# Transposes by the DMA crossbar in place of TensorE: a linear-attention and gated-FFN kernel on one core

## The chip, the core and the metric

The kernel runs on one core of a Trainium2 chip. The core has a matrix engine (TensorE, PE in the profile), a vector engine (VectorE, DVE), an activation engine (ScalarE, ACT), a general engine (GpSimd, POOL) and a queue engine (SyncE, SP) that issues most transfers; sixteen DMA engines carry them. TensorE writes to the accumulation memory PSUM, from which VectorE or ScalarE must copy; everything else lives in the on-chip memory SBUF. The metric is the device time of one execution in microseconds.

## The reference

Eight heads of a recurrent attention with a decay per head, over four sequences of 768 tokens, then an RMS norm and a gated feed-forward layer (3072 tokens, 512 wide, 1536 inside):

```python
gamma = 1.0 - 2.0 ** (-5.0 - np.arange(H))          # H = 8, D = 64, S = 768, B = 4
for t in range(S):
    state = gamma * state + einsum('bhd,bhe->bhde', k[:, :, t], v[:, :, t])
    y[:, :, t] = (1 / sqrt(D)) * einsum('bhd,bhde->bhe', q[:, :, t], state)
x = y.transpose(0, 2, 1, 3).reshape(B * S, H * D)
xn = x / sqrt(mean(x * x) + 1e-6) * rms_g
g = xn @ w_gate
out = (g / (1 + exp(-g)) * (xn @ w_val)) @ w_out
```

## The kernel before

The sequence is cut into six chunks of 128 tokens. A chunk has four batch rows (b), each a tile of 128 tokens by 512 (eight heads of 64). For one chunk and row the attention is a series of pieces:

- `cast` (L136): q and k from float32 to bfloat16, and v times a decay per token, on GpSimd (q of chunk 0 on VectorE). After it, from chunk 1 on, SP issues the loads of the next chunk's same row (L149).
- `piece_t` (L152): q and k must have the head dimension on the partitions for the scores. Eight TensorE transposes of 128x128 write them to PSUM, and one ScalarE copy brings them back (L159).
- `piece_a` (L163): scores of all heads on TensorE; VectorE masks them on the way out (L173).
- `piece_y` (L178): masked scores times v, plus q times the running state; the update of the state; the output's decay on VectorE (L200), its squares on ScalarE (L204), the inverse norm on GpSimd (`piece_rstd`, L220).
- `piece_n` (L228): the row times its inverse norm, to bfloat16, on VectorE.
- `piece_x` (L234): four TensorE transposes of that row into PSUM; VectorE copies them into the tile `xnT` and multiplies by the gain `rms_g`, which in this layout is one value per partition (L239).

When all four rows of a chunk stand in `xnT`, its FFN (`ffn`, L261) runs in 16 slots: twelve gate/value slots (`gv`: four matmuls each with the two weight matrices, a SiLU on ScalarE, a product on VectorE) and four output slots (`down`: twelve matmuls, a ScalarE copy, a store issued by SP).

The order of the work is written out by hand: every engine runs its instructions in program order. The last loop (L305 to L313) walks through the 16 slots of chunk c's FFN and puts into each slot the attention pieces of chunk c + 1 that a table assigns to it: `PLAN` (L247), or `PLAN1` (L248) for chunk 1. For example `a=(2, 4, 6, 8)` puts the scores of rows 0 to 3 into slots 2, 4, 6 and 8. The prologue (L294 to L304) does the whole attention of chunk 0, with the loads of the weights between. The loads of chunk 1 go out in the first four slots of chunk 0's FFN, each held back until a SiLU of that slot is done.

Buffers: `loads` (L46) has six per tensor, one per chunk and row; `work` (L47) three, unless a tile says otherwise; PSUM is split between attention (`aps`, four) and FFN (`fps`, four). Output copies have three buffers (`ffw`, L48).

Of the kernel before, what the change touches and what calls it, by code (L numbers as in the profile page):

```python
# [9 lines left out]
F32 = mybir.dt.float32  # L10
BF16 = mybir.dt.bfloat16
AX = mybir.AxisListType
AF = mybir.ActivationFunctionType
ALU = mybir.AluOpType
# [3 lines left out]
def kernel(  # L18
# [11 lines left out]
    nc = tc.nc  # L30
    ctx.enter_context(tc.manual_schedule())

    B, H, S, D = q.shape
    C = 128
    NCH = S // C
    NHP = H // 2
    DM = H * D
# [5 lines left out]
    lng = [math.log(1.0 - 2.0 ** (-5.0 - h)) for h in range(H)]  # L43

    const = ctx.enter_context(tc.tile_pool(name="const", bufs=1))
    loads = ctx.enter_context(tc.tile_pool(name="loads", bufs=6))  # L46
    work = ctx.enter_context(tc.tile_pool(name="work", bufs=3))  # L47
    ffw = ctx.enter_context(tc.tile_pool(name="ffw", bufs=3))  # L48
    aps = ctx.enter_context(tc.tile_pool(name="aps", bufs=4, space=bass.MemoryType.PSUM))
# [10 lines left out]
    def load(c, b, after=None):  # L60
        t = []
        for name, src in (("q_f", q), ("k_f", k), ("v_f", v)):
            x = loads.tile([128, H, D], F32, name=name)
            i = nc.sync.dma_start(  # L64
                out=x, in_=src[b].rearrange("h (c p) d -> c p h d", p=C)[c])
            if after is not None:
                tc.add_manual_dep(i.ins, after.ins.name, SYNC_DEP, reason="transfer order")
            t.append(x)
        raw[c, b] = t

    for b in range(B):
# [8 lines left out]
        out=causal, in_=causal, compare_op=ALU.is_ge, fill=0.0, base=0,  # L80
# [19 lines left out]
    nc.scalar.activation(warm, zero, AF.Silu)  # L100
    g_col = const.tile([128, KS], F32, name="g_col")

    def load_g():
        with nc.allow_non_contiguous_dma(reason="one column per 128 entries"):
            nc.gpsimd.dma_start(out=g_col, in_=moe_rms_g.rearrange("(s p) -> p s", p=128))
# [27 lines left out]
    cur = {}  # L133
    mark = {}

    def cast(c, b):  # L136
        q_f, k_f, v_f = raw.pop((c, b))
        qb = work.tile([128, DM], BF16, name="qb")
        kb = work.tile([128, DM], BF16, name="kb")
        vp = work.tile([128, H, D], BF16, name="vp")  # L140
        if c == 0:
            nc.vector.tensor_copy(qb, q_f.rearrange("p h d -> p (h d)"))
        else:
            nc.gpsimd.tensor_copy(qb, q_f.rearrange("p h d -> p (h d)"))  # L144
        nc.gpsimd.tensor_copy(kb, k_f.rearrange("p h d -> p (h d)"))  # L145
        nc.gpsimd.tensor_tensor(  # L146
            out=vp, in0=v_f, in1=vdec[:, c, :, None].to_broadcast([128, H, D]), op=ALU.mult)
        cur[c, b] = dict(qb=qb, kb=kb, vp=vp)
        if 0 < c < NCH - 1:  # L149
            load(c + 1, b)  # L150

    def piece_t(c, b):  # L152
        d = cur[c, b]
        qk_ps = aps.tile([128, 2, NHP, 128], BF16, name="qk_ps", tag="at")
        for i, n in enumerate(("qb", "kb")):
            for hp in range(NHP):
                nc.tensor.transpose(qk_ps[:, i, hp, :], d[n][:, hp * 128:(hp + 1) * 128], ident)  # L157
        qkT = work.tile([128, 2, NHP, 128], BF16, name="qkT")
        nc.scalar.copy(qkT, qk_ps)  # L159
        d["qT"] = qkT[:, 0]  # L160
        d["kT"] = qkT[:, 1]
# [66 lines left out]
    def piece_n(c, b):  # L228
        d = cur[c, b]
        xn = work.tile([128, DM], BF16, name="xn")  # L230
        nc.vector.tensor_scalar_mul(xn, d["x"].rearrange("p h d -> p (h d)"), d["rstd"])  # L231
        d["xn"] = xn

    def piece_x(c, b):  # L234
        xn = cur.pop((c, b))["xn"]
        xt_ps = aps.tile([128, KS, 128], BF16, name="xt_ps", tag="at")
        for s in range(KS):
            nc.tensor.transpose(xt_ps[:, s, :], xn[:, s * 128:(s + 1) * 128], ident)  # L238
        nc.vector.tensor_tensor(  # L239
            out=cur[c, "xnT"][:, :, b * C:(b + 1) * C], in0=xt_ps,  # L240
            in1=g_col[:, :, None].to_broadcast([128, KS, 128]), op=ALU.mult)

    def begin(c):
        cur[c, "xnT"] = work.tile([128, KS, GT], BF16, name="xnT", bufs=2)


    PLAN = dict(cast=(0, 2, 4, 6), t=(1, 3, 5, 7), a=(2, 4, 6, 8), y=(3, 5, 7, 9), n=(6, 8, 10, 13), x=(7, 9, 11, 14))  # L247
    PLAN1 = dict(cast=(5, 7, 9, 11), t=(7, 9, 11, 13), a=(8, 10, 12, 14), y=(9, 11, 13, 15), n=(12, 14, 15, 15), x=(13, 15, 15, 15))  # L248

    def attention(c):  # L250
        s = [[] for _ in range(16)]
        s[0].append(lambda: begin(c))
        plan = PLAN1 if c == 1 else PLAN
        pieces = dict(cast=cast, t=piece_t, a=piece_a, y=piece_y, n=piece_n, x=piece_x)
        for b in range(B):
            for n, f in pieces.items():
                s[plan[n][b]].append(lambda f=f, b=b: f(c, b))
        return s


    def ffn(c):  # L261
        xnT = cur.pop((c, "xnT"))
        hT = ffw.tile([128, NFF, GT], BF16, name="hT", bufs=2)
        slots = []

        def gv(n):
            sl = slice(n * 128, (n + 1) * 128)
            g_ps = fps.tile([128, GT], F32, name="g_ps", tag="ff")
            for s in range(KS):
                nc.tensor.matmul(g_ps, wg_b[:, s, sl], xnT[:, s, :], start=s == 0, stop=s == KS - 1)  # L270
            v_ps = fps.tile([128, GT], F32, name="v_ps", tag="ff")
            for s in range(KS):
                nc.tensor.matmul(v_ps, wv_b[:, s, sl], xnT[:, s, :], start=s == 0, stop=s == KS - 1)  # L273
            sg = ffw.tile([128, GT], BF16, name="sg")
            mark[c, n] = nc.scalar.activation(sg, g_ps, AF.Silu)  # L275
            nc.vector.tensor_tensor(out=hT[:, n, :], in0=sg, in1=v_ps, op=ALU.mult)  # L276

        def down(b):
            o_ps = fps.tile([128, DM], F32, name="o_ps", tag="ff")
            for n in range(NFF):  # L280
                nc.tensor.matmul(o_ps, hT[:, n, b * C:(b + 1) * C], wo_b[:, n, :],  # L281
                                 start=n == 0, stop=n == NFF - 1)
            o_sb = ffw.tile([128, DM], F32, name="o_sb")
            nc.scalar.copy(o_sb, o_ps)  # L284
            nc.sync.dma_start(out=out_v[c, b], in_=o_sb)

        for n in range(NFF):
            slots.append(lambda n=n: gv(n))
        for b in range(B):
            slots.append(lambda b=b: down(b))  # L290
        return slots


    begin(0)  # L294
    P = dict(C=cast, T=piece_t, A=piece_a, Y=piece_y, N=piece_n, X=piece_x, W=lambda c, i: load_w(i), G=lambda c, i: load_g())
    for step in ("C0 T0 C1 G0 A0 T1 Y0 C2 W0 W1 A1 T2 Y1 N0 C3 W2 W3 A2 X0 T3 Y2 N1 A3 X1 Y3 N2 X2").split():
        P[step[0]](0, int(step[1]))
# [3 lines left out]
    for i in range(6):  # L301
        nc.tensor.matmul(hot, ident, st_b[0].rearrange("p a b -> p (a b)"), start=True, stop=True)
    piece_n(0, 3)
    piece_x(0, 3)  # L304
    for c in range(NCH):  # L305
        f_slots = ffn(c)
        a_slots = attention(c + 1) if c + 1 < NCH else [[] for _ in range(16)]
        for i in range(16):
            f_slots[i]()
            if c == 0 and i < B:  # L310
                load(1, i, after=mark[0, i])
            for f in a_slots[i]:
                f()  # L313

# [29 lines left out]
```

## Time and profile before

| | us |
|---|---|
| median of 3 runs | 279.93 (279.19 to 281.76) |
| the profiled execution | 279.49 |
| its span, first to last instruction | 277.8 |
| mean granted TensorE clock | 0.988 |

A profile comes from one execution. Times in its rows are microseconds from the start of the span; `L270` is line 270 of the kernel. A row of a group gives busy time and the mean length of one instruction, then how long the engine had stood idle before and what ended that wait. `PEld` is the loading of weights into TensorE, which overlaps its matmuls. Matmul lengths contain the pipeline's tail, so the distance between starts is what one costs. For SP the length of a DMA instruction is how long it held the queue; the landing is a column of its own. The chain of waits goes back from the last instruction, at each step to what released it.

### The profile page before, as it was taken

How to read it: one execution, taken by the hardware profiler on the slowest of the kernel's cores; microseconds unless marked ns; L12 is line 12 of the kernel's file. 1: busy time of each engine (PE TensorE's matmuls, PEld its weight loads, DVE VectorE, ACT ScalarE, POOL GpSimd, SP SyncE). 2: the span in 40 equal slices, each digit the busy share in tenths (PEclk: the TensorE clock that was granted, in tenths of full speed). 3: DMA queues.
4: the chain of work that ended last, by engine and by line, in shares of the span. 5: the costliest groups of instructions: out<-in, count | busy, mean ns of one | idle time of the engine just before them, and what ended most of it. 6: DMA issues, size and time to landing. Idle time of an engine off the chain costs nothing.

```text
span 277.8 us, 4510 instructions
## 1 busy us (share of the span) xinstructions
PE 246.2 (89%) x1702; PEld 124.4 (45%) x1702; DVE 135.7 (49%) x228; ACT 105.3 (38%) x203; POOL 94.5 (34%) x177
## 2 busy tenths in 40 slices
PE   1567899999299989999989999989999889999994
PEld 0344344455244544445454445544444444444441
DVE  0547134755616778117778027777036664023300
ACT  8546133433124432243432244333144333143311
POOL 6698104662342735303726204627104411000000
PEclk9999999999869999999999999999999999999999
DMA  8999999999898000149900279700200000200012
GB/s 160 218 179 203 204 196 223 212 226 199 246 222 169 0 2 0 76 126 223 182 2 1 108 164 220 119 1 2 113 38 2 0 2 0 113 38 4 0 58 93
DMA packets 84197, 30.17 MB, mean 109 GB/s; under 512 B 75472, under 2 KB 81104, under 8 KB 84176
## 3 DMA queue, kind: packets, MB, share of 16 engines
q1 hardware_dynamic: 78336, 25.17, 42.8%
q0 software_dynamic: 5840, 4.72, 11.0%
q8 instruction: 13, 0.21, 0.4%
q14 instruction: 8, 0.07, 0.1%
HBM read 28.31 MB, written 6.29 MB: 125 GB/s over the span
## 4 chain that ended last, share of the span: by engine, by line
PE 51%; DVE 15%; ACT 9%; DMA 8%; POOL 6%; issue 6%; SPq 3%; ACTq 0%; POOLq 0%; DVEq 0%
PE o_ps L281 21%; PE g_ps L270 13%; PE v_ps L273 12%; DVE am L173 5%; DMA k_f<-in_k_dram 4%; DVE hT L276 3%; SPq L64 3%; ACT xsq L204 3%; DVE x L200 3%; ACT qkT L159 3%; ACT sg L275 3%; DVE xn L231 2%; DMA v_f<-in_v_dram 2%; DVE xnT L239 2%; PE xt_ps L238 2%
## 5 line engine op out<-in xcount | busy, mean ns | idle before, releaser
L276 DVE TENSOR_TENSOR hT<-sg,v_ps 128x512 bf16<-128x512 bf16 x72 | 49.4, 686 | 80.3 <-PE v_ps L273 55.4
L270 PE MATMUL g_ps<-xnT,wg_b 128*128 128x512 bf16 x288 | 76.3, 388 | 1.6 <-DVE xnT L239 1.6
L273 PE MATMUL v_ps<-xnT,wv_b 128*128 128x512 bf16 x288 | 75.7, 386 | 0.0
L275 ACT ACTIVATE sg<-g_ps 128x512 bf16<-128x512 f32 x72 | 43.0, 597 | 59.9 <-PE g_ps L270 59.9
L281 PE MATMUL o_ps<-wo_b,hT 128*128 128x512 bf16 x288 | 64.3, 379 | 0.0
L273 PEld LDWEIGHTS <-wv_b 128*128 128x128 bf16 x288 | 28.6, 99 | 35.3 <-issue 2.2
L222 POOL TENSOR_SCALAR ms<-ssq 128x1 f32<-128x1 f32 x24 | 5.1, 212 | 111.3 <-ACT xsq L204 111.2
L281 PEld LDWEIGHTS <-hT 128*128 128x128 bf16 x288 | 27.6, 98 | 31.4
L270 PEld LDWEIGHTS <-wg_b 128*128 128x128 bf16 x288 | 26.3, 100 | 29.5 <-issue 4.7
L284 ACT COPY o_sb<-o_ps 128x512 f32<-128x512 f32 x24 | 14.1, 586 | 55.6 <-PE o_ps L281 50.5
L173 DVE TENSOR_TENSOR am<-a_ps,causal 128x512 bf16<-128x512 f32 x48 | 30.8, 682 | 3.7 <-PE a_ps L169 3.7
L239 DVE TENSOR_TENSOR xnT<-xt_ps,g_col 128x512 bf16<-128x512 bf16 x24 | 16.5, 686 | 30.9 <-PE xt_ps L238 30.9
L204 ACT ACTIVATE xsq<-x 128x512 f32<-128x512 f32 x24 | 15.1, 630 | 42.7 <-DVE x L200 42.4
L159 ACT COPY qkT<-qk_ps 128x1024 bf16<-128x1024 bf16 x24 | 24.0, 999 | 10.2 <-PE qk_ps L157 10.2
L146 POOL TENSOR_TENSOR vp<-v_f,vdec 128x512 bf16<-128x512 f32 x24 | 24.9, 1039 | 2.3 <-DMA v_f<-in_v_dram 2.3
L200 DVE TENSOR_TENSOR x<-y_ps,ydec 128x512 f32<-128x512 f32 x24 | 16.4, 684 | 5.1 <-PE y_ps L186 5.0
L144 POOL CAST qb<-q_f 128x512 bf16<-128x512 f32 x20 | 12.8, 640 | 15.0 <-DMA q_f<-in_q_dram 14.1
L186 PE MATMUL y_ps<-vp,am 128*128 128x64 bf16 x192 | 13.1, 202 | 4.5 <-DVE am L173 4.5
L145 POOL CAST kb<-k_f 128x512 bf16<-128x512 f32 x24 | 15.2, 635 | 4.5 <-DMA k_f<-in_k_dram 4.5
L169 PE MATMUL a_ps<-qkT 64*128 64x128 bf16 x192 | 10.4, 233 | 6.7 <-ACT qkT L159 6.1
L231 DVE TENSOR_SCALAR xn<-x,rstd 128x512 bf16<-128x512 f32 x24 | 15.6, 649 | 1.1 <-POOL rstd L225 1.1
L238 PE MATMUL xt_ps<-ident,xn 128*128 128x128 bf16 x96 | 10.5, 238 | 5.4 <-DVE xn L231 5.4
(43 smaller groups left out, 159.7 us busy)
## 6 DMA issues: line engine op xcount, KB each, us to landing
q_f<-in_q_dram SPq DMA_DIRECT2D x24, 256.0 KB, 5.1
k_f<-in_k_dram SPq DMA_DIRECT2D x24, 256.0 KB, 5.0
v_f<-in_v_dram SPq DMA_DIRECT2D x24, 256.0 KB, 5.1
out_dram<-o_sb SPq DMA_DIRECT2D x24, 256.0 KB, 2.0
wg_b<-in_moe_w_gate_dram POOLq DMA_DIRECT2D x4, 384.0 KB, 8.3
wv_b<-in_moe_w_val_dram POOLq DMA_DIRECT2D x4, 384.0 KB, 9.1
wo_b<-in_moe_w_out_dram POOLq DMA_DIRECT2D x3, 512.0 KB, 13.2
g_col<-in_moe_rms_g_dram POOLq DMA_DIRECT2D x1, 2.0 KB, 4.2
```

The lines of the kernel that those rows point to most:

```text
L146: nc.gpsimd.tensor_tensor(out=vp, in0=v_f, in1=vdec[:, c, :, None].to_broadcast([128, H, D]), op=ALU.mult)
L159: nc.scalar.copy(qkT, qk_ps)
L173: nc.vector.tensor_tensor(out=am[:, i], in0=a_ps[i], in1=causal[:, None, :].to_broadcast([128, NHP, 128]), op=ALU.mult)
L200: nc.vector.tensor_tensor(out=x, in0=y_ps, in1=ydec[:, c, :, None].to_broadcast([128, H, D]), op=ALU.mult)
L204: nc.scalar.activation(xsq, x.rearrange("p h d -> p (h d)"), AF.Square, accum_out=ssq)
L231: nc.vector.tensor_scalar_mul(xn, d["x"].rearrange("p h d -> p (h d)"), d["rstd"])
L239: nc.vector.tensor_tensor(out=cur[c, "xnT"][:, :, b * C:(b + 1) * C], in0=xt_ps, in1=g_col[:, :, None].to_broadcast([128, KS, 128]), op=AL ...
L270: nc.tensor.matmul(g_ps, wg_b[:, s, sl], xnT[:, s, :], start=s == 0, stop=s == KS - 1)
L273: nc.tensor.matmul(v_ps, wv_b[:, s, sl], xnT[:, s, :], start=s == 0, stop=s == KS - 1)
L275: mark[c, n] = nc.scalar.activation(sg, g_ps, AF.Silu)
L276: nc.vector.tensor_tensor(out=hT[:, n, :], in0=sg, in1=v_ps, op=ALU.mult)
L281: nc.tensor.matmul(o_ps, hT[:, n, b * C:(b + 1) * C], wo_b[:, n, :], start=n == 0, stop=n == NFF - 1)
```

## The change

From chunk 2 on, q and k are not transposed on TensorE: right after the casts, SP issues two DMA transposes through the crossbar, from the cast tile in SBUF to a transposed tile in SBUF. `piece_t` does nothing there, and the PSUM tile and the ScalarE copy fall away. From chunk 1 on, the normalised row goes the same way: `piece_n` multiplies by the inverse norm and by the gain in one VectorE instruction (`scalar_tensor_tensor`), and SP issues a transpose straight into `xnT`; `piece_x` does nothing there. For this the gain is needed along the free dimension on all partitions, so a tile `g_bc` is loaded once by a broadcast, in slot 4 of the first FFN stage. Chunk 0, and q and k of chunk 1, stay as they were.

The tables change: all four casts come in slots 0 to 3 and the scores from slot 4 on. The loads go out two chunks ahead, in slots 5, 7, 9 and 11, no longer from `cast`. Load buffers go from six to eight, those of the cast tiles from three to six.

```diff
-    loads = ctx.enter_context(tc.tile_pool(name="loads", bufs=6))
+    loads = ctx.enter_context(tc.tile_pool(name="loads", bufs=8))
...
+    g_bc = const.tile([128, DM], F32, name="g_bc")
...
-        qb = work.tile([128, DM], BF16, name="qb")
-        kb = work.tile([128, DM], BF16, name="kb")
-        vp = work.tile([128, H, D], BF16, name="vp")
+        qb = work.tile([128, DM], BF16, name="qb", bufs=6)
+        kb = work.tile([128, DM], BF16, name="kb", bufs=6)
+        vp = work.tile([128, H, D], BF16, name="vp", bufs=6)
...
-        if 0 < c < NCH - 1:
-            load(c + 1, b)
+        if c > 1:
+            d = cur[c, b]
+            for n in "qk":
+                t = work.tile([128, NHP, 128], BF16, name=n + "T", bufs=6)
+                nc.sync.dma_start_transpose(out=t, in_=d[n + "b"])
+                d[n + "T"] = t
 
     def piece_t(c, b):
+        if c > 1:
+            return
...
         xn = work.tile([128, DM], BF16, name="xn")
-        nc.vector.tensor_scalar_mul(xn, d["x"].rearrange("p h d -> p (h d)"), d["rstd"])
+        x = d["x"].rearrange("p h d -> p (h d)")
+        if c > 0:
+            nc.vector.scalar_tensor_tensor(out=xn, in0=x, scalar=d["rstd"], in1=g_bc,
+                                           op0=ALU.mult, op1=ALU.mult)
+            nc.sync.dma_start_transpose(out=cur[c, "xnT"][:, :, b * C:(b + 1) * C], in_=xn)
+            return
+        nc.vector.tensor_scalar_mul(xn, x, d["rstd"])
...
     def piece_x(c, b):
-        xn = cur.pop((c, b))["xn"]
+        d = cur.pop((c, b))
+        if c > 0:
+            return
+        xn = d["xn"]
...
-    PLAN = dict(cast=(0, 2, 4, 6), t=(1, 3, 5, 7), a=(2, 4, 6, 8), y=(3, 5, 7, 9), n=(6, 8, 10, 13), x=(7, 9, 11, 14))
-    PLAN1 = dict(cast=(5, 7, 9, 11), t=(7, 9, 11, 13), a=(8, 10, 12, 14), y=(9, 11, 13, 15), n=(12, 14, 15, 15), x=(13, 15, 15, 15))
+    PLAN = dict(cast=(0, 1, 2, 3), t=(1, 3, 5, 7), a=(4, 6, 8, 10), y=(5, 7, 9, 11), n=(7, 9, 11, 13), x=(8, 10, 12, 14))
+    PLAN1 = dict(cast=(5, 7, 9, 11), t=(7, 9, 11, 13), a=(8, 10, 12, 14), y=(9, 11, 13, 15), n=(11, 13, 15, 15), x=(13, 15, 15, 15))
...
             if c == 0 and i < B:
                 load(1, i, after=mark[0, i])
+            if c == 0 and i == 4:
+                nc.sync.dma_start(out=g_bc, in_=moe_rms_g.partition_broadcast(128))
+            if c < NCH - 2 and i in (5, 7, 9, 11):
+                load(c + 2, (i - 5) // 2)
```

## The prediction

> **What bounds the kernel now.** I read the page first, then busy time by stage, then what TensorE waits for in the stages, then the chain of waits around the one stage boundary that looks different. The page:
>
> ```profile
> span 277.8 us, 4510 instructions
> ...
> PE 246.2 (89%) x1702; PEld 124.4 (45%) x1702; DVE 135.7 (49%) x228; ACT 105.3 (38%) x203; POOL 94.5 (34%) x177
> ...
> PE 51%; DVE 15%; ACT 9%; DMA 8%; POOL 6%; issue 6%; SPq 3%; ACTq 0%; POOLq 0%; DVEq 0%
> ```
>
> TensorE is busy for 89% and holds half of the chain that ended last. The span cut at the first gate matmul of each chunk (start to end, length, busy time of PE, PEld, DVE, ACT and POOL with instruction counts, granted clock, DMA share, GB/s) gives the prologue, five FFN stages that carry the next chunk's attention, and the last FFN alone:
>
> ```profile
> core 0: us, PE busy (x) PEld busy (x) DVE busy (x) ACT busy (x) POOL busy (x), PEclk, DMA share, GB/s
> 0.00:29.43 29.43, 15.59 (x135) 10.06 (x136) 13.58 (x24) 17.51 (x47) 22.36 (x45) 1.00 1.21 191
> 29.43:76.31 46.88, 41.05 (x289) 20.59 (x289) 23.33 (x40) 15.83 (x28) 16.55 (x30) 0.97 1.08 216
> 76.31:119.55 43.24, 41.46 (x289) 20.65 (x289) 23.44 (x40) 15.02 (x27) 18.23 (x33) 0.95 0.38 82
> 119.55:160.52 40.97, 39.19 (x289) 20.07 (x288) 23.43 (x40) 15.60 (x28) 15.06 (x28) 1.00 0.50 104
> 160.52:201.49 40.97, 39.19 (x289) 20.07 (x288) 23.43 (x40) 15.60 (x28) 15.06 (x28) 1.00 0.51 104
> 201.49:243.10 41.61, 38.61 (x273) 19.10 (x272) 20.21 (x32) 15.60 (x28) 7.22 (x14) 1.00 0.07 26
> 243.10:277.80 34.70, 31.08 (x144) 13.88 (x142) 8.26 (x12) 10.09 (x17) 0.00 (x0) 1.00 0.10 38
> ```
>
> In stages 1 to 4 (I number them by the chunk whose FFN runs, 0 to 4) TensorE is busy 39.19 of 40.97 us, VectorE only 23.43 and the DMA engines half. A TensorE instruction taken out there is time off the stage, as long as its replacement arrives in time. Stage 0 is another matter: the DMA share is above 1, so it is fed by transfers. What TensorE waited for between 76 and 250 us (total, times, longest):
>
> ```profile
> PE a_ps L169 <- ACT qkT L159: 3.9, 9, 0.7
> PE y_ps L186 <- DVE am L173: 3.8, 13, 0.4
> ...
> PE xt_ps L238 <- DVE xn L231: 0.3, 2, 0.2
> ```
>
> The first and third of these disappear with the instructions that the change removes; the second, the masked scores, stays.
>
> **The change part by part.** *TensorE transposes.* For one batch row in stage 3, four transposes of q, four of k, then the next gate matmul; and four of the normalised row, then the next matmul (start, length):
>
> ```profile
> 168.86 0.39 PE L157 MATMUL qk_ps<-ident,qb 128*128 128x128 bf16 x4
> ...
> 169.08 0.39 PE L157 MATMUL qk_ps<-ident,kb 128*128 128x128 bf16 x4
> ...
> 169.30 1.03 PE L270 MATMUL g_ps<-xnT,wg_b 128*128 128x512 bf16 x4
> ...
> 190.51 0.40 PE L238 MATMUL xt_ps<-ident,xn 128*128 128x128 bf16 x4
> ...
> 190.74 7.93 PE L281 MATMUL o_ps<-wo_b,hT 128*128 128x512 bf16 x36
> ```
>
> The lengths contain the pipeline's tail; the real price is the distance between starts: 0.22 us for q, 0.22 for k, 0.23 for the normalised row, so 0.67 us per row and 4 x 0.67 = 2.7 us per stage. Stages 1 to 4 (chunks 2 to 5) lose all three: 4 x 2.7 = 10.8 us. With them go the waits for the PSUM copy of q and k, 3.9 us, and for the normalised rows, 0.3. Sum: 15.0 us off stages 1 to 4. Chunk 1 loses only its normalised rows' transposes, 4 x 0.23 = 0.9 us in stage 0, which buys nothing because that stage ends on transfers (below).
>
> *VectorE and ScalarE.* The scaling by the gain moves from the PSUM copy into the normalisation:
>
> ```profile
> L239 DVE TENSOR_TENSOR xnT<-xt_ps,g_col 128x512 bf16<-128x512 bf16 x24 | 16.5, 686 | 30.9 <-PE xt_ps L238 30.9
> L200 DVE TENSOR_TENSOR x<-y_ps,ydec 128x512 f32<-128x512 f32 x24 | 16.4, 684 | 5.1 <-PE y_ps L186 5.0
> ...
> L231 DVE TENSOR_SCALAR xn<-x,rstd 128x512 bf16<-128x512 f32 x24 | 15.6, 649 | 1.1 <-POOL rstd L225 1.1
> ```
>
> A fused two-operand form has no row here; I price it as the two-operand instruction of the same size, 684 ns, at most the sum 649 + 686 and at least 649. VectorE so loses about 0.65 us per row, and ScalarE loses the q/k copy. Neither engine is the bound; priced at nothing, beyond the waits counted above.
>
> *What a crossbar transpose costs.* Nothing in this trace shows one. Each moves 128 KB; stages 1 to 4 get 12 each (8 for q and k, 4 for normalised rows), all issued by SP, which also issues loads and stores. The nearest rows:
>
> ```profile
> q1 hardware_dynamic: 78336, 25.17, 42.8%
> ...
> q_f<-in_q_dram SPq DMA_DIRECT2D x24, 256.0 KB, 5.1
> ...
> out_dram<-o_sb SPq DMA_DIRECT2D x24, 256.0 KB, 2.0
> ```
> ```profile
> 32.99 5.62 SPq L64 DMA_DIRECT2D v_f<-in_v_dram  x1
> ...
> 121.15 2.51 SPq L64 DMA_DIRECT2D k_f<-in_k_dram  x1
> ...
> 161.21 0.33 SPq L285 DMA_DIRECT2D out_dram<-o_sb  x1
> 161.63 0.39 SPq L64 DMA_DIRECT2D q_f<-in_q_dram  x1
> ...
> 173.60 1.10 SPq L64 DMA_DIRECT2D v_f<-in_v_dram  x1
> ```
>
> A store into idle queues holds SP 0.33 us and lands in 2.0 us; twelve loads hold it from 161.63 to 174.70, 1.09 us each, and land in 5.1 us because they queue; the longest hold once the weights are in is 2.51 us, and 5.62 while they still come. By packets: 42.8% of 16 engines' 277.8 us over 78,336 packets is 24 ns each, so 128 KB in 256-byte pieces (512) would take 512 x 24 / 16 = 0.8 us of all engines. I take a hold of 1.1 us (between 0.33 and 2.51, nearest to the queued load; 5.62 only with queues as full as then) and a landing of 3.0 us: the store's 2.0 plus 1.0 for a 256 KB store just ahead of it (ends 2.0 and 5.1).
>
> The Trainium skill's "VectorE: DVE Perf Modes", The three transpose paths, speaks against the change: it lists 1309 ns for one 128x128 block by the DMA crossbar against 390 ns on TensorE; four blocks would make an estimated 5.2 us per transpose, and what that does to the time is rival D's far end. The trace already differs on TensorE, where blocks follow each other at 0.22 / 4 = 0.055 us. "Advanced Engine Details and Errata", X-Bar Transpose (TRN2), says the opposite, that such transfers run as fast as ordinary ones; no run here shows either yet.
>
> *Is it hidden?* For q and k: the casts on GpSimd now run ahead, with six buffers. At present a pair of rows is cast while the previous stage's down projection still runs:
>
> ```profile
> 190.78 0.61 POOL L144 CAST qb<-q_f 128x512 bf16<-128x512 f32 x1
> ...
> 194.22 1.04 POOL L146 TENSOR_TENSOR vp<-v_f,vdec 128x512 bf16<-128x512 f32 x1
> ...
> 196.12 0.59 ACT L284 COPY o_sb<-o_ps 128x512 f32<-128x512 f32 x1 [2.00 <-PE o_ps L281]
> ...
> 201.32 1.03 PE L270 MATMUL g_ps<-xnT,wg_b 128*128 128x512 bf16 x4
> ```
>
> Two rows took 190.78 to 195.26, so four take 9.0 us, ready about when the stage ends. Their eight transposes sit on SP behind the previous stage's last store, about 1 us into the stage. The first scores now come in slot 4, after five gate/value pairs of 8 x 0.216 = 1.73 us (31.08 us for 144 matmuls is 0.216 each): 8.6 us. The first pair lands at 1 + 2 x 1.1 + 3.0 = 6 us, the others gain on their slots. Hidden; without that cover one pair would cost up to its 5.2 us. Loads for two chunks ahead have free buffers and follow on SP.
>
> For the normalised rows: the last row's transpose (slot 13) stands on SP behind the store of that slot, which waits for the ScalarE copy that starts at 196.12 and ends at 196.71. The next stage's first matmul is at 201.32; after 0.4 us for the store's issue 4.2 us remain, against a landing of 3.0. Hidden, by 1.2 us only.
>
> *Stage 0* has no such slack. Its chain now:
>
> ```profile
> 66.84 1.00 SPq L64
> ...
> 67.93 3.99 DMA out_dram<-o_sb
> ...
> 74.27 0.60 DVE xn L231
> ...
> 75.56 0.70 DVE xnT L239
> ...
> 76.31 1.01 PE g_ps L270 x2
> ```
>
> SP is still issuing loads until 67.84; the first store lands at 71.92, the fourth output copy waits for that buffer, and behind it on ScalarE stand the squares of the last row, then its norm. The change puts two more transfers ahead of that store on SP: the broadcast gain (256 KB, like a load 1.1) and the first normalised row's transpose (1.1). That delays all by 2.2 us. At the end 76.31 - 74.87 = 1.44 us of TensorE transpose and copy become a landing of 3.0: +1.6. Together +3.8 us; ends 0.33 + 0.33 + 0.6 = 1.3 and 1.1 + 2.5 + 3.7 = 7.3.
>
> *Sum.* -15.0 + 3.8 = -11.2 us. The profiled execution took 279.49 us (span 277.8), 0.44 below the median of 279.93: 279.49 - 11.2 = **268.3 us**, a span of 266.6.
>
> **The rivals.** *A, the stage ends are exposed.* If a transpose lands in the load's 5.1 us, each of stages 1 to 4 ends 0.9 us late and stage 0 another 2.1: +5.7, 274.0 us. For: only 1.2 us of slack; against: the queues are nearly idle then. *B, the waits move.* The waits for the masked scores grow by what the others lost, so only the 10.8 us of TensorE work count: 10.8 - 3.8 = 7.0 off, 272.5 us. For: VectorE's instructions still separate scores and output; against: it loses 0.65 us per row. *C, A and B together with a dearer stage 0* (its 7.3 in place of 3.8 includes A's 2.1 there): -10.8 + 3.6 + 7.3 = +0.1, 279.6 us, no change.
>
> *D, slower: the transfer queue becomes the bound.* With 12 loads and 4 stores at 1.09 us (17.4) and 12 transposes at X, stages 1 to 3 take 17.4 + 12X. This passes my stage of about 37.2 us (40.97 - 15.0 / 4) at X = 1.65 us and today's 41 at 1.97. At X = 2.51, the longest hold above, a stage takes 47.5: +4.3, +6.5, +6.5; stage 4 has no loads (34.5, hidden) and keeps its -3.8; stage 0 pays 1.1 + 2.5 + 3.7 = 7.3. Sum +20.8, 300 us. For: SP is in order, so a slow transpose also holds back loads and stores; against: 0.8 us by the packets' rate. The longer the hold the worse: at 5.62 us stages 1 to 3 take 84.8 and stage 4 71.8: 41.6 + 43.8 + 43.8 + 30.2 plus, in stage 0, 1.1 + 5.6 + 3.7 = 10.4, is +170, near 449 us. The page's 1309 ns times four, 5.2 us, lies near that end, and by it the time would be an estimated 429 us.
>
> **How the numbers follow.** Forecast 0.50 (266 to 271), A 0.13, B 0.11, C 0.08, D 0.18 (of it 0.04 for a hold near 5 us). Runs of this kernel spread by about 1%, so I call under 1% no change: forecast, A and B are faster (0.74), C the same (0.08), D slower (0.18). The low end is 264: stage 0 at 1.3 in place of 3.8 (265.8) and about half of the 3.8 us of waits for the masked scores gone too. The high end, 280, takes in C and leaves D out; the faster cases' own range is 264 to 275.
>
> **What would show it.** Right: stages 1 to 4 near 37 us with no TensorE wait on a transfer over 0.5 us; transposes holding SP about 1.1 us and landing in about 3; stage 0 ending near 80 us; the granted clock still low just after it. Wrong: TensorE waiting in the scores (line 169) or at a stage's first gate matmul for a transpose in every stage (A, D), SP busy through whole stages (D), or waits of line 186 grown to 8 us (B).

## The result, and the profile after

The changed kernel takes 267.56 us (median; 266.61 to 267.91), the kernel before 279.58 beside it: a ratio of 0.955, 95% interval 0.9493 to 0.9606. The forecast was 268.3 us. The profiled execution took 266.61 us, the shortest of the four.

The page of the changed kernel, in the lines shown for before:

```profile
span 264.9 us, 4103 instructions
...
PE 231.2 (87%) x1467; PEld 112.6 (42%) x1494; DVE 124.8 (47%) x208; ACT 91.0 (34%) x187; POOL 93.9 (35%) x177
...
PE 59%; DVE 12%; DMA 11%; ACT 4%; POOL 4%; SPq 4%; issue 4%; DVEq 0%; ACTq 0%; POOLq 0%
```

The span cut into stages (columns as in the prediction):

```profile
29.48:80.18 50.70, 39.52 (x268) 19.60 (x272) 21.87 (x36) 15.71 (x28) 17.77 (x32) 0.98 1.05 207
80.18:119.50 39.32, 38.34 (x237) 17.94 (x242) 21.08 (x36) 11.47 (x23) 19.06 (x36) 0.94 0.71 141
119.50:156.46 36.96, 35.92 (x236) 17.33 (x240) 21.08 (x36) 12.06 (x24) 14.78 (x29) 1.00 0.82 157
156.46:193.48 37.02, 35.94 (x237) 17.34 (x240) 21.09 (x36) 12.06 (x24) 14.82 (x30) 1.00 0.83 157
193.48:230.00 36.52, 35.20 (x220) 16.43 (x224) 17.91 (x28) 12.06 (x24) 5.08 (x12) 1.00 0.29 73
```

Stages 1 to 4 lost 3.9, 4.0, 4.0 and 5.1 us, 17.0 together; stage 0 gained 3.8 (46.88 to 50.70); prologue and last stage moved by 0.05 and 0.2. By these two traces the span fell by 12.9 us (277.8 to 264.9), by the medians the time fell by 12.0; 11.2 were forecast. The DMA share of stages 2 and 3 rose from 0.50 to 0.82. The granted clock was still low just after stage 0, as forecast: 0.50 from 80.18 to 84.18 us. What TensorE waited for from 80 to 232 us (total, times, longest), and what the DMA issues show (KB where known, median landing):

```profile
PE g_ps L287 <- DMA xnT<-xn: 7.5, 1, 7.5
PE y_ps L194 <- DVE am L181: 3.2, 9, 0.4
```
```profile
out_dram<-o_sb SPq DMA_DIRECT2D x24, 256.0 KB, 2.1
...
xnT<-xn SPq DMA_TRANSPOSE x20, 2.4
...
qT<-qb SPq DMA_TRANSPOSE x16, 2.5
kT<-kb SPq DMA_TRANSPOSE x16, 2.4
```

The only wait for a transpose is the one at the end of stage 0. SP in stage 3, whose first gate matmul starts at 156.29 and the next stage's at 193.28 (start, hold):

```profile
157.57 1.22 SPq L155 DMA_TRANSPOSE qT<-qb  x1
...
166.88 1.22 SPq L155 DMA_TRANSPOSE kT<-kb  x1
...
189.36 1.23 SPq L243 DMA_TRANSPOSE xnT<-xn  x1
```

Eight transposes of q and k go out between 157.57 and 168.10, one every 1.33 us; the last row's goes out at 189.36 and lands 2.4 us later, 1.5 us before the next stage needs it. The end of stage 0, in order of time:

```profile
68.78 1.01 SPq L64 DMA_DIRECT2D v_f<-in_v_dram  x1
...
69.89 1.68 SPq L243 DMA_TRANSPOSE xnT<-xn  x1
...
71.67 1.00 SPq L302 DMA_DIRECT2D out_dram<-o_sb  x2
...
74.62 0.59 ACT L301 COPY o_sb<-o_ps 128x512 f32<-128x512 f32 x1 [5.00 <-DMA out_dram<-o_sb]
75.10 0.63 ACT L212 ACTIVATE xsq<-x 128x512 f32<-128x512 f32 x1
...
75.66 3.26 SPq L243 DMA_TRANSPOSE xnT<-xn  x2
...
76.85 0.85 DVE L241 SCALAR_TENSOR_TENSOR xn<-x,rstd,g_bc 128x512 bf16<-128x512 f32 x1 [2.86 <-POOL rstd L233]
...
80.18 1.44 PE L287 MATMUL g_ps<-xnT,wg_b 128*128 128x512 bf16 x3 [7.47 <-DMA xnT<-xn]
```

The fourth output copy stands on ScalarE until the first store has landed, and the last row's squares behind it, as before; now the store itself goes out 3.7 us later, and at the end TensorE waits for a transfer.

### The profile page after: what moved, and what is told of

It reads as the page before. It is cut to its first block, busy times and chain, and to the rows that moved or that the text cites. A ratio compares the mean times of both kernels' runs of the same rounds, so it can differ in the third digit from the quotient of the medians.

```text
span 264.9 us, 4103 instructions
## 1 busy us (share of the span) xinstructions
PE 231.2 (87%) x1467; PEld 112.6 (42%) x1494; DVE 124.8 (47%) x208; ACT 91.0 (34%) x187; POOL 93.9 (35%) x177
## 4 chain that ended last, share of the span: by engine, by line
PE 59%; DVE 12%; DMA 11%; ACT 4%; POOL 4%; SPq 4%; issue 4%; DVEq 0%; ACTq 0%; POOLq 0%
PE o_ps L298 21%; PE g_ps L287 16%; PE v_ps L290 15%; DMA k_f<-in_k_dram 5%; SPq L64 4%; DVE hT L293 4%; DVE am L181 4%; ACT sg L292 2%; DVE xn L241 2%; DMA g_bc<-in_moe_rms_g_dram 2%; DMA v_f<-in_v_dram 2%; PE a_ps L177 2%; DVE x L208 2%; PE y_ps L194 1%; ACT xsq L212 1%
## 5 line engine op out<-in xcount | busy, mean ns | idle before, releaser
L287 PE MATMUL g_ps<-xnT,wg_b 128*128 128x512 bf16 x275 | 75.2, 390 | 8.7 <-DMA xnT<-xn 7.5
L298 PE MATMUL o_ps<-wo_b,hT 128*128 128x512 bf16 x281 | 63.1, 379 | 0.5 <-issue 0.2
L212 ACT ACTIVATE xsq<-x 128x512 f32<-128x512 f32 x24 | 15.1, 630 | 45.8 <-DVE x L208 45.6
L241 DVE SCALAR_TENSOR_TENSOR xn<-x,rstd,g_bc 128x512 bf16<-128x512 f32 x20 | 15.5, 776 | 9.9 <-POOL rstd L233 7.8
L146 POOL CAST qb<-q_f 128x512 bf16<-128x512 f32 x20 | 12.2, 610 | 14.5 <-DMA q_f<-in_q_dram 14.1
L194 PEld LDWEIGHTS <-am 128*128 128x128 bf16 x192 | 9.4, 104 | 12.6 <-DVE am L181 11.1
L225 POOL CAST st_b<-st_f 64x256 bf16<-64x256 f32 x32 | 14.0, 439 | 0.9
L233 POOL TENSOR_TENSOR rstd<-ms,mhalf 128x1 f32<-128x1 f32 x24 | 13.2, 552 | 2.0
L224 DVE TENSOR_TENSOR st_f<-st_f,kv_ps 64x256 f32<-64x256 f32 x32 | 13.2, 413 | 0.5
```

The lines of the kernel that those rows point to most:

```text
L194: nc.tensor.matmul(y_ps[:, h, :], d["am"][:, i, hp, :], d["vp"][:, h, :], start=first, stop=last, skip_group_check=True)
L212: nc.scalar.activation(xsq, x.rearrange("p h d -> p (h d)"), AF.Square, accum_out=ssq)
L241: nc.vector.scalar_tensor_tensor(out=xn, in0=x, scalar=d["rstd"], in1=g_bc, op0=ALU.mult, op1=ALU.mult)
```

## The experiments

The theory: in stages 1 to 4 TensorE is the bound, so what is taken off it, with the waits around it, is time, and the transposes are hidden; stage 0 pays for what is added ahead of its stores and at its end. The rivals: the gain comes from the new order and the earlier loads; or SP or the DMA engines are close to being the bound. A ratio is against the kernel before timed beside that run (medians from 279.58 to 280.80 us). The start of stage 1 and the length of stage 3, from the first gate matmuls in each trace:

| kernel | us (median) | ratio, 95% interval | stage 1 starts | stage 3 |
|---|---|---|---|---|
| before | 279.58 | | 76.31 | 40.97 |
| changed | 267.56 | 0.955 (0.9493 to 0.9606) | 80.18 | 36.99 |
| e4, order only | 277.38 | 0.9894 (0.9865 to 0.9923) | 77.30 | 40.63 |
| e1, rows by crossbar, q and k not | 277.88 | 0.9915 (0.9885 to 0.9944) | 81.12 | 39.53 |
| e2, q and k by crossbar, rows not | 267.47 | 0.9545 (0.9519 to 0.9571) | 77.05 | 38.10 |
| e3, rows from chunk 2 on | 263.61 | 0.9413 (0.9386 to 0.9441) | 77.53 | 37.00 |

**e4, the order alone.** The conditions for the crossbar (`c > 1` in `cast` and `piece_t`, `c > 0` in `piece_n` and `piece_x`) are out of reach, and the broadcast gain is not loaded.

```diff
-        if c > 1:
+        if c > 5:
...
-        if c > 0:
+        if c > 5:
...
-            if c == 0 and i == 4:
-                nc.sync.dma_start(out=g_bc, in_=moe_rms_g.partition_broadcast(128))
```

> No crossbar transpose at all: the new tables, the loads two chunks ahead and the buffers, with all transposes on TensorE. Theory: TensorE has all its work back, 4 x 2.7 us, and only the waits for the PSUM copy may shrink, since scores now come three slots after the transposes: 276 to 280 us. Rival (the order brings the gain): near 268 us.

277.38 us. The order brings about 1% by itself: 0.3 us in each of stages 2 and 3 and 1.2 in stage 4. The rival falls. No wait for the PSUM copy is left between 84 and 245 us, but the waits for the masked scores have grown (under e2).

**e1, only the rows by the crossbar.** In `cast` and `piece_t`:

```diff
-        if c > 1:
+        if c > 5:
```

> q and k of every chunk back on TensorE, in the changed order; normalised rows still by the crossbar. Theory (what is taken off TensorE is time off the stage, and the waits for the PSUM copy go with it): each of stages 1 to 4 gets 4 x 0.45 = 1.8 us of transposes back, 274.8 us in all, and up to 278.7 if the waits of 3.9 us come back too; with the scores three slots behind the transposes I expect about half of them. Rival (the gain comes from the new order, the early loads and casts): no change, 267.6 us.

277.88 us, near the upper end: 3.1 of the 3.9 us beyond the transposes came back, but not as the theory had it. No wait for the PSUM copy is in the trace from 84 to 245 us; those for the masked scores are longer there, 5.9 us where the changed kernel has 3.2 (the reason is under e2):

```profile
PE y_ps L194 <- DVE am L181: 5.9, 17, 0.5
```

Against e4 the rows take 1.1 us off stage 3 and put 3.8 on the start of stage 1, 81.12 for 77.30: together nothing.

**e2, only q and k by the crossbar.** The first pair of lines in `piece_n` and in `piece_x`:

```diff
-        if c > 0:
+        if c > 5:
...
-            if c == 0 and i == 4:
-                nc.sync.dma_start(out=g_bc, in_=moe_rms_g.partition_broadcast(128))
```

> Normalised rows of every chunk back on TensorE with the VectorE copy, no broadcast gain; q and k still by the crossbar. Theory: stages 1 to 4 get 4 x 0.23 = 0.9 us each back, +3.7, and stage 0 loses its +3.8 us: 267.5 us, no change, with stage 0 about 47 us long. Rival (stage 0 is long for another reason, the earlier loads): about 271 us with stage 0 still near 50.7 us.

267.47 us, no change against the changed kernel, and stage 0 ends at 77.05: as the theory had it. Against e4, q and k take 2.5 us off stage 3, of which 4 x 0.45 = 1.8 are the transposes on TensorE. The other 0.7 show in the waits between 84 and 245 us; e4 first, then e2:

```profile
PE y_ps L194 <- DVE am L181: 6.5, 17, 0.6
```
```profile
DVE hT L293 <- ACT sg L292: 16.3, 12, 2.2
```
```profile
PE y_ps L194 <- DVE am L181: 3.4, 9, 0.4
```
```profile
DVE hT L293 <- ACT sg L292: 9.0, 12, 1.3
```

With the q/k copy on ScalarE, the SiLU of the next slot stands behind it, VectorE's product behind the SiLU, the masked scores behind the product, and TensorE behind these. One instance in e4:

```profile
134.40 0.99 ACT L167 COPY qkT<-qk_ps 128x1024 bf16<-128x1024 bf16 x1
...
135.29 0.60 ACT L292 ACTIVATE sg<-g_ps 128x512 bf16<-128x512 f32 x1
...
135.93 0.69 DVE L293 TENSOR_TENSOR hT<-sg,v_ps 128x512 bf16<-128x512 bf16 x1 [1.47 <-ACT sg L292]
...
136.53 1.28 DVE L181 TENSOR_TENSOR am<-a_ps,causal 128x512 bf16<-128x512 f32 x2
...
137.87 0.38 PE L194 MATMUL y_ps<-vp,am 128*128 128x64 bf16 x7 [0.40 <-DVE am L181]
```

That is what the order of the instructions and these waits say; no run takes the copy off ScalarE and leaves the transposes on TensorE, so its part is not shown alone.

**e3, the rows by the crossbar from chunk 2 on.** Chunk 1 keeps TensorE for its rows, so stage 0 has neither the gain nor a transpose on SP; the first pair of lines again in `piece_n` and `piece_x`.

```diff
-        if c > 0:
+        if c > 1:
...
-            if c == 0 and i == 4:
+            if c == 1 and i == 4:
```

> Normalised rows by the crossbar only from chunk 2 on, the broadcast gain loaded one stage later; all else as in the changed kernel. Theory: stage 0 goes back to about 46.9 us, stages 1 to 4 stay at 37: 267.6 - 3.8 = 263.8 us. Rival (the earlier loads of chunk 2 make stage 0 long): 267.6 us.

263.61 us, faster than the changed kernel with intervals that do not touch. Stage 0 is shorter again, 47.98 us, and stages 2 to 4 are as in the changed kernel. The profiled execution took 265.20 us, the longest of six, so this trace shows less of the gain than the medians do. Stage 1 starts at:

```profile
77.53 1.86 PE L287 MATMUL g_ps<-xnT,wg_b 128*128 128x512 bf16 x4 [0.78 <-DVE xnT L256]
```

**e5, q and k transposed twice**, the first time into a tile that nobody reads.

```diff
             for n in "qk":
+                tx = work.tile([128, NHP, 128], BF16, name="tx", bufs=6)
+                nc.sync.dma_start_transpose(out=tx, in_=d[n + "b"])
                 t = work.tile([128, NHP, 128], BF16, name=n + "T", bufs=6)
```

> Each q and k transpose is issued twice, the first time into a tile that nobody reads, so 20 transposes a stage in place of 12. Theory (SP's order and holds of about 1.3 us with gaps decide, and there is slack): the scores of row 0 still find their data (1 + 4 x 1.31 + 1.2 = 7.4 us against 8.6), those of row 3 just (23.2 against 23.7), but 20 x 1.3 + 12 x 0.9 + 4 x 0.4 = 38.4 us of SP in a stage of 37 makes stages 1 to 3 longer by 1.5 to 2: 268 to 273 us. Rival (a transpose costs only its landing, SP is free meanwhile): 267.6 us.

283.87 us, ratio 1.0113 (1.0068 to 1.0158): slower than before by about 1%, and well above what was expected. SP runs through stage 1 with hardly a gap, and TensorE waits at the stage ends (SP first, then TensorE; the first of the two waits ends with an output copy, the second with a row's transpose):

```profile
78.71 1.22 SPq L157 DMA_TRANSPOSE tx<-qb  x1
...
99.46 1.26 SPq L158 DMA_TRANSPOSE kT<-kb  x1
...
118.84 1.22 SPq L246 DMA_TRANSPOSE xnT<-xn  x1
...
121.84 1.22 SPq L157 DMA_TRANSPOSE tx<-qb  x1
```
```profile
121.81 1.87 PE L290 MATMUL g_ps<-xnT,wg_b 128*128 128x512 bf16 x4 [2.75 <-ACT o_sb L304]
...
165.28 1.89 PE L290 MATMUL g_ps<-xnT,wg_b 128*128 128x512 bf16 x4 [4.77 <-DMA xnT<-xn]
```

From one stage's first transpose to the next's are 43.1 us. The sixteen of q and k take 22.0; the other 21.1 go to loads (10.5), row transposes (6.7), stores (2.6) and gaps (1.2), where the expectation had 10.8, 5.2, 1.6 and none. The loads were priced right; too cheap were the row transposes, three of which stand right behind loads and hold SP 1.8 to 1.9 us, and the stores. The sum written for rival D in the prediction, 17.4 us for loads and stores plus the transposes at 1.3, gives 43.4. Four matmuls take 1.87 us after the first of these waits, where 1.03 is usual; the granted clock was 0.50 from 121.81 to 124.00 us.

**e6 and e11, three times.** The added transpose stands there twice. The kernel is the same in both. Of e6's four executions three took 323.94 to 324.29 us; the fourth, the profiled one, took 823.04 us, for a reason that its trace does not show. So e11 gave the profile that is read here.

> Each q and k transpose is issued three times, 28 transposes a stage. Theory (the transfer queue becomes the bound): 28 x 1.3 + 10.8 + 1.6 = 48.8 us of SP in stages 1 to 3, 11.8 more than now, and in stage 4 the scores of row 3 wait until 1 + 24 x 1.31 + 1.2 = 33.6 us in place of 23.7: 267.6 + 3 x 11.8 + 9.9 = 313 us. Rival (SP is not what a transpose holds): under 275 us.

> Each q and k transpose three times, once more, for its profile. Theory (SP's order is the bound): about 324 us, with SP issuing without a gap through stages 1 to 3, some 24 x 1.3 + 4 x 1.75 + 11.3 + 2.8 = 52 us each by the holds seen with two, and TensorE waiting at the first gate matmul and at the scores. Rival (the DMA engines' own throughput is the bound): SP would show holds well above 1.3 us for these transposes.

e6 took 324.18 us, ratio 1.1566 (1.152 to 1.1613), above the 313 for the reasons that e5 showed; e11 324.48. TensorE's waits from 70 us on, and SP's holds (two of the extra transposes in one row), in e11:

```profile
PE a_ps L180 <- DMA kT<-kb: 28.3, 12, 3.9
PE g_ps L290 <- DMA xnT<-xn: 11.2, 2, 6.2
PE g_ps L290 <- ACT o_sb L304: 10.4, 2, 5.2
```
```profile
79.10 2.53 SPq L157 DMA_TRANSPOSE tx<-qb  x2
81.69 1.25 SPq L158 DMA_TRANSPOSE qT<-qb  x1
```

Nearly all holds of q and k stay at 1.21 to 1.27 us, as with one. In stage 2 the transposes of q and k fill SP from 133.79 to 166.05 us and the loads, stores and row transposes the rest (columns as in the prediction):

```profile
133.73:166.00 32.27, 25.88 (x160) 11.82 (x160) 16.71 (x28) 8.40 (x17) 4.11 (x12) 0.89 0.55 104
166.00:187.00 21.00, 14.93 (x80) 7.10 (x80) 5.19 (x8) 3.67 (x7) 10.97 (x17) 0.88 1.20 212
```

With a DMA share of 0.55, what is full in the first stretch is SP's order and not the DMA engines. In the second the share is 1.20: there the DMA engines are full too, and the row transposes behind loads hold SP 1.76 to 1.93 us. Stages 2 and 3 (from 133.73 to 187.20 and on to 241.53) last 53.5 and 54.3 us; 17.4 + 28 x 1.3 is 53.8.

**e7, the last row one slot later.**

```diff
-    PLAN = dict(cast=(0, 1, 2, 3), t=(1, 3, 5, 7), a=(4, 6, 8, 10), y=(5, 7, 9, 11), n=(7, 9, 11, 13), x=(8, 10, 12, 14))
+    PLAN = dict(cast=(0, 1, 2, 3), t=(1, 3, 5, 7), a=(4, 6, 8, 10), y=(5, 7, 9, 11), n=(7, 9, 11, 14), x=(8, 10, 12, 14))
```

> In the table of chunks 2 to 5 the last normalised row moves from slot 13 to slot 14, one store later on SP. Theory (the last row's transpose has about 1.5 us of slack before the next stage, and one output slot is 2.6 us): each of stages 1 to 4 ends 1.1 us late, 267.6 + 4.4 = 272 us, with TensorE waiting at the first gate matmul. Rival (there is more slack than the issue times show): 267.6 us.

271.56 us (0.9694; 0.966 to 0.9729). Each of four stage ends waits 1.0 us:

```profile
PE g_ps L287 <- DMA xnT<-xn: 3.9, 4, 1.0
```

So the transpose of the last row was hidden, with 1.5 us to spare and no more.

**e8, four output buffers.**

```diff
-            o_sb = ffw.tile([128, DM], F32, name="o_sb")
+            o_sb = ffw.tile([128, DM], F32, name="o_sb", bufs=4)
```

> Four buffers for the output copies in place of three, nothing else. Theory (in stage 0 the fourth copy waits for the first store to land, and the last row's squares stand behind it): the squares start about 1.9 us earlier, then the order on SP decides (two more transposes behind the last store, landing at about 78.6 us in place of 80.1): 267.6 - 1.5 = 266.1 us. Rival (SP's order alone decides the end of stage 0): 267.6 us.

265.99 us, 0.9485 (0.9456 to 0.9514), an interval that overlaps the changed kernel's. The trace goes the theory's way: stage 1 starts 1.0 us earlier, and TensorE still waits for the last transpose.

```profile
79.22 1.01 PE L287 MATMUL g_ps<-xnT,wg_b 128*128 128x512 bf16 x2 [6.45 <-DMA xnT<-xn]
```

**e9, the gain loaded early**, from GpSimd's queue behind the weights.

```diff
     for i in range(3):
         load_wo(i)
+    nc.gpsimd.dma_start(out=g_bc, in_=moe_rms_g.partition_broadcast(128))
...
-            if c == 0 and i == 4:
-                nc.sync.dma_start(out=g_bc, in_=moe_rms_g.partition_broadcast(128))
```

> The changed kernel with the broadcast gain loaded from GpSimd's queue in the prologue, behind the weights, in place of SP's slot 4. Theory (what stands ahead of the stores on SP decides the end of stage 0): 1.15 us less on SP ahead of the first store, 267.6 - 1.1 = 266.4 us. Rival (the DMA engines are full there, so the same 256 KB only come earlier and push the loads back as much): no change, 267.6 us.

266.07 us, 0.9468 (0.9435 to 0.9502), overlapping the changed kernel's interval by a little. SP's last load ends at 69.35 us for 69.79, and stage 1 starts at 79.64 for 80.18: half of what SP's order would give. The run does not decide; both may have a part. In the changed kernel the gain lands 5.5 us after its issue, and VectorE's first row waits 2.1 us for it, which the prediction left out. In e9 that wait is gone, and TensorE still waits 7.3 us at the end of stage 0, for 7.5 in the changed kernel.

**e10, both together**: e3 with four output buffers.

> Normalised rows by the crossbar from chunk 2 on (gain loaded in stage 1), and four output buffers. Theory: without the wait for the first store the squares of the last row in stage 0 start when its row is ready, 0.9 us earlier than with three buffers: 263.6 - 0.9 = 262.7 us. Rival: the wait is covered, 263.6 us.

264.08 us, 0.9401 (0.9369 to 0.9433), against 0.9413 (0.9386 to 0.9441) for e3. Stage 1 starts at 76.83 instead of 77.53, but the two cannot be told apart by time. Both beat the changed kernel by about 1.5%.

## Why the prediction was right, point by point

*TensorE's transposes are time off stages 1 to 4: right.* 2.7 us per stage were forecast for TensorE's work alone. The crossbar shortens stage 3 by 40.63 - 36.99 = 3.6 against the same order without it, 2.5 for q and k and 1.1 for the rows.

*The waits that go with them: about right in size, for another reason.* The prediction took off the 3.9 us for the PSUM copy and let the 3.8 for the masked scores stand. In e4 the first disappear, because the scores come later, but the second grow to 6.5: the mechanism of rival B, as long as the copy sits on ScalarE. With q and k by the crossbar they come down, to 3.4 in e2 and 3.2 in the changed kernel; the likely cause is that the copy in front of the SiLU is gone from ScalarE, which is argued from the order of the work and not shown by a run of its own. The prediction priced ScalarE's lost copy at nothing; that was the mis-sized term. Stages 1 to 4 gave 17.0 us for the forecast 15.0. The order alone gave 1.8 of them (these stages last 164.8 us in e4 and 166.6 before), which the sum left out, and the crossbar 15.1. That this meets the 15.0 is in part luck, since the waits it took away are not those of the sum.

*The price of a transpose: right.* A hold of 1.22 us for the assumed 1.1, a landing of 2.4 to 2.5 for 3.0. The four blocks of a transpose hold SP 1.22 us together and land in 2.4. The Trainium skill's "VectorE: DVE Perf Modes", The three transpose paths, lists 1309 ns for one 128x128 block; these cannot be added up block by block here, and the estimated 5.2 us was four times the hold and twice the landing. The Trainium skill's "Advanced Engine Details and Errata", X-Bar Transpose (TRN2), says that they run as fast as ordinary transfers. That fits the landing only roughly (2.4 us for 128 KB, where a 256 KB store takes 2.1), and not the queue: 1.22 us of hold for the 0.33 that an unhindered store took.

*Hidden: right.* Slack at the stage end was 1.2 by the prediction and 1.5 in the trace; e7 used it up. The scores never waited for q or k.

*Stage 0: right in sum by luck, not in its parts.* Forecast were +2.2 ahead of the store and +1.6 at the end. The last load ended 1.95 us later (69.79 for 67.84) and the first transpose held SP 1.68, so the store went out 3.7 us late; but it landed sooner, and the last row was normalised 2.8 us late (77.70 for 74.87). From there to the first matmul were 2.5 us in place of 1.44, +1.0 rather than +1.6. The errors cancel: stage 1 starts 3.9 us later (80.18 for 76.31), for the forecast 3.8. Nor is all of it the price of the rows and their gain. In e4, e2 and e3, which have neither in stage 0, the last load still ends at 68.51 to 69.05 and stage 1 starts at 77.05 to 77.53, about 1 us after the kernel before; whether the new order or the spread between executions makes this 1 us stays open. By the starts of stage 1, rows and gain cost 3.8 us between e4 and e1 and 3.1 between e2 and the changed kernel; leaving chunk 1's rows on TensorE (e3) brought 4.0 us by the medians.

*Rival D: not the case, but its sum holds.* 17.4 + 12 x 1.3 is 33 us, below the stage's 37; the holds in stage 3 of the changed kernel add up to 27. With 20 and 28 transposes the queue is the bound, and the sum, 43.4 and 53.8, meets the measured 43.1 and 53.5 to 54.3. That close a match is luck: in e5 loads and stores took 13.2 us of SP where the sum has 17.4, the transposes 28.7 where it has 26, and 1.2 were gaps. A, C and the far end of D did not occur.

## What to carry to other kernels

When one engine fills a stage, look at what else the removed step used: here shorter waits, most likely because the PSUM copy no longer stood in front of the SiLU on ScalarE, were about a quarter of what q and k by the crossbar brought. A queue with room is a resource like an engine: add up the holds of everything on it per stage, with the holds seen when it is full, before giving it more. Where a stage ends on transfers, leave the work on the engine that waits there anyway: the same edit brought 1.1 us in each later stage and cost 3.1 to 3.8 in that one.

## What was not expected of the hardware

The hold of a transpose was 1.19 to 1.27 us in most rows, with one, two or three per tile, and 1.7 to 1.9 right behind loads. In stage 3 of the changed kernel the first two loads behind a row's transpose held SP 0.58 us each; twelve loads in a row in the kernel before came 1.09 us apart. The fused VectorE instruction with two float32 operands and a per-row scalar took 776 ns on average, above the 684 of the two-operand one.
